# Column sums of exp(phi) by VectorE in place of a block of ones, with a list of side units for each period

## The chip, the cores and the metric

The kernel runs on one core of one Trainium2 chip. The metric is the device time of one execution in microseconds, the median of several runs. Before the change it is 239.88 us (three runs, 239.66 to 240.74).

The core has a matrix engine (TensorE, PE in the profile; its weight loads are PEld), a vector engine (VectorE, DVE), a scalar engine (ScalarE, ACT), GpSimd (POOL) and DMA queues. Matmul results go to PSUM, which this kernel manages as eight banks.

## What is computed

Attention with 32 memory slots for each of 8 batches and 8 heads, and then a bilinear feed-forward layer over all 4608 tokens:

```python
def _attn_ref(q, k, v, phi):                     # q, k, v: (8, 8, 576, 64); phi: (8, 8, 576, 32)
    a = phi - np.max(phi, axis=2, keepdims=True)
    a = np.exp(a)
    a = a / (np.sum(a, axis=2, keepdims=True) + 1e-09)
    k_m = np.einsum('bhsm,bhsd->bhmd', a, k)
    v_m = np.einsum('bhsm,bhsd->bhmd', a, v)
    scores = scale * np.matmul(q, k_m.transpose(0, 1, 3, 2))
    ...                                          # softmax over the 32 slots
    return np.matmul(attn, v_m)

def _moe_ref(x, w_a, w_b, w_out):                # 4608 x 512, d_ff = 1536
    return (x @ w_a) * (x @ w_b) @ w_out
```

The softmax over the sequence (axis 2) divides by the column sums of exp(phi). These are the sums that the change computes in another way.

## The kernel before

The 576 tokens of a batch are laid out as 64 partitions times NI = 9 blocks, with two heads one above the other on the 128 partitions, so NHP = 4 head pairs. `exp_phi` (L194, two halves z) makes exp(phi) in float16. `kv_sums` (L205 to L219) multiplies it with k, v and a third block, which was filled once with 1/16 (`kv_sb`, 2 buffers by batch parity, third index 0 k, 1 v, 2 ones). Each of its 72 matmuls uses a 64x32 tile of the array and 192 columns: 64 for k, 64 for v, and 64 equal ones for the column sums; eight tiles work side by side. `take_kv` (L228, L233) takes the reciprocal of one of these columns and scales k_m and v_m into `rep`. A DMA transpose (`kv_turn`) or TensorE (`kv_transpose`) makes `kvT`. From it `scores` (L297, 32x32 tiles) and `fold` (L368, 64x32 tiles) work: fold multiplies v_m into the two first weight matrices, a third of the 1536 columns at a time (v0, v1, v2), and `take_fold` (L381) copies the results to `vab`, by ScalarE and VectorE. Batches 0 and 1 use a separate path (`sums`, L260), which the change leaves alone.

The long loop is `ups`: for each batch, in two halves of tokens, 12 blocks of d_ff. `up_half` (L633) makes pa and pb (two matmuls of 288 columns each); ScalarE copies pa to `a_sb` (L641), VectorE multiplies it with pb into `ht` (L644). So a batch has 24 slots, a "period". After each slot come two things: `work.advance()`, which pulls some matmuls of the down projection (py, pv, px, L505; written as seven products for two token blocks, on sums `h_sums` that GpSimd makes, L487), at a rate planned for each half, and one entry of a list of side units. These are written out by hand as strings: units joined by + run in one slot, - is an empty slot, a prime means the next batch and _ the one before. The names: exp0/exp1 exp_phi; qt0 to qt3 transposes of q on VectorE (L203); kv and km0/km1 `kv_sums` and `take_kv`; kvt, kvd the transposes; sc, e0, e1 scores and their exponentials; ed, sm0, sm1, tn0, tn1, ad the normalisation by tokens (from batch 4); den, nr the other normalisation; v0, x0a, x0b `fold` and `take_fold` of the first third; L a load of inputs two batches ahead of the one named in the list; d3 means that three more matmuls of the down projection are pulled here.

In period b the unprimed units belong to batch b + 1 and the primed ones to batch b + 2. Before, period 2 has its own list, periods 3 to 5 share one (`every`), period 6 has `last`, and period 7 none.

PSUM banks are handed out in the order in which they were freed; scores, fold and kv_sums hold theirs (4, 4 and 2) until they have been read. Before sc and v0, `settle` pulls down-projection matmuls until one of their banks is free. Each engine executes its own instructions in order, and the loads are issued from GpSimd's queue.

Of the kernel before, what the change touches and what calls it, by code (L numbers as in the profile page):

```python
# [8 lines left out]
F32 = mybir.dt.float32  # L9
F16 = mybir.dt.float16  # L10
AF = mybir.ActivationFunctionType
ALU = mybir.AluOpType

P = 128
CS = 16.0
# [3 lines left out]
def kernel(  # L19
# [11 lines left out]
    nc = tc.nc  # L31

    B, H, S, D = q.shape
    M = phi.shape[3]
    d_model, d_ff = moe_w_a.shape
    NHP = H // 2
# [6 lines left out]
    consts = ctx.enter_context(tc.tile_pool(name="consts", bufs=1))  # L43
# [29 lines left out]
    phis, qs, kvs = {}, {}, {}  # L73
    kv_sbs = [consts.tile([P, 3, NHP, NI * D], F16, name=f"kv_sb{t}") for t in range(2)]

    def load_phi(b):
        phis[b] = inp.tile([P, NHP, NI * M], F32, name="phi_sb")
        nc.gpsimd.dma_start(out=phis[b], in_=rows(phi, b))

    def load_k(b, hps=slice(0, NHP)):  # L80
        kvs[b] = kv_sbs[b % 2]
        nc.gpsimd.dma_start(out=kvs[b][:, 0, hps], in_=rows(k, b)[:, hps])

    def load_v(b, hps=slice(0, NHP)):
        nc.gpsimd.dma_start(out=kvs[b][:, 1, hps], in_=rows(v, b)[:, hps])

    def load_q(b, hps=slice(0, NHP)):
        if b not in qs:
            qs[b] = inp.tile([P, NHP, NI * D], F16, name="q_sb")
        nc.gpsimd.dma_start(out=qs[b][:, hps], in_=rows(q, b)[:, hps])  # L90

    def load(b):
        load_phi(b)
        load_k(b)
        load_v(b)
        load_q(b)
# [48 lines left out]
    banks = Banks()  # L145
# [29 lines left out]
    for x in "o0 o1 p k q0 o2 o3 q1 v0 v1 o4 o5".split():  # L175
        loads[x]()

    attn = {}
    vabs = {}

    def head(g, j):

        jj = j ^ g
        return jj % 2, 2 * g + jj // 2

    def units(b):

        u = {}
        t = {}
# [10 lines left out]
        def q_transpose(hp):  # L200
            if hp == 0:
                t["qT"] = mid.tile([P, NHP, NI * D], F16, name="qT")
            nc.vector.transpose(out=t["qT"][:, hp, :].bitcast(F32), in_=qs[b][:, hp, :].bitcast(F32))  # L203

        def kv_sums():  # L205

            t["pkv"] = [banks.take([P, 3, D], F32, "pkv", hold=True) for _ in range(2)]
            for i in range(NI):
                for g in range(2):
                    for j in range(4):  # L210
                        r, hp = head(g, j)
                        nc.tensor.matmul(  # L212
                            t["pkv"][g][0][32 * j:32 * j + 32],
                            t["exp"][64 * r:64 * r + 64, hp, i, :],
                            kvs[b][64 * r:64 * r + 64, :, hp, D * i:D * (i + 1)],
                            start=(i == 0),
                            stop=(i == NI - 1),
                            tile_position=(64 * r, 32 * j),
                        )  # L219

        def take_kv(gs=range(2)):

            if gs[0] == 0:
                t["rep"] = mid.tile([P, 6, P], F16, name="rep")
                t["rphi"] = small.tile([P, 2], F32, name="rphi")
            for g in gs:
                pkv, bank = t["pkv"][g]
                nc.vector.reciprocal(out=t["rphi"][:, g:g + 1], in_=pkv[:, 2, 0:1])  # L228
                km = pkv[:, 0].rearrange("p (d e) -> p e d", e=2).unsqueeze(2).to_broadcast([P, 2, 4, 32])
                vm = pkv[:, 1].unsqueeze(1).to_broadcast([P, 2, D])  # L230
                for out, x in ((t["rep"][:, 2 * g:2 * g + 2].rearrange("p e (z d) -> p e z d", z=4), km),
                               (t["rep"][:, 4 + g].rearrange("p (z d) -> p z d", z=2), vm)):
                    nc.vector.tensor_scalar(out=out, in0=x, scalar1=t["rphi"][:, g:g + 1], scalar2=None, op0=ALU.mult)  # L233
                banks.free(bank)
# [149 lines left out]
        def one(f, *a):  # L384
            return lambda: f(*a)

        for z in range(2):
            u[f"exp{z}"] = one(exp_phi, z)
            u[f"ks{z}"] = one(sums, z, 0)
            u[f"kt{z}"] = one(transpose, z, 0)  # L390
            u[f"vs{z}"] = one(sums, z, 1)
            u[f"vt{z}"] = one(transpose, z, 1)
            u[f"s{z}"] = one(scores, (z,))
            u[f"e{z}"] = one(exp_scores, z)
            u[f"km{z}"] = one(take_kv, (z,))
            u[f"den{z}"] = one(denominators, z)
            u[f"nr{z}"] = one(normalise, z)
            for hf in range(2):
                u[f"den{z}{hf}"] = one(denominators, z, (hf,))
                u[f"nr{z}{hf}"] = one(normalise, z, slice(hf, hf + 1))  # L400
            for n in range(NCH):
                u[f"v{n}{'ab'[z]}"] = one(fold, 512 * n, 512 * (n + 1), (z,))
                u[f"x{n}{'ab'[z]}"] = one(take_fold, 512 * n, 512 * (n + 1), z)
            for n in range(2):
                u[f"hv{n}{'ab'[z]}"] = one(fold, 256 * n, 256 * (n + 1), (z,))
                u[f"hx{n}{'ab'[z]}"] = one(take_fold, 256 * n, 256 * (n + 1), z)
        for n in range(NCH):
            u[f"v{n}"] = one(fold, 512 * n, 512 * (n + 1), (0, 1))
        for x in range(4):
            u[f"qt{x}"] = one(q_transpose, x)  # L410
        u["sc"] = one(scores, (0, 1))
        u["kv"] = one(kv_sums)
        u["km"] = one(take_kv)
        u["kvt"] = one(kv_transpose)
        u["kvd"] = one(kv_turn)
# [230 lines left out]
    def up(b, i, hfs):  # L646
        for hf in hfs:
            up_half(b, i, hf, 0)
        if len(hfs) > 1:
            yield  # L650
        for hf in hfs:
            up_half(b, i, hf, 1)
        yield

    def ups(steps, side=()):

        side = iter(side)
        for step in steps:
            for _ in up(*step):
                work.advance()  # L660
                next(side, us[step[0]]["-"])()
        for f in side:
            work.advance()
            f()
# [5 lines left out]
    def half_steps(b, hf, lo=0):  # L670

        return [(b, i, (hf,)) for i in range(lo, NFF)]

    us = {b: units(b) for b in range(B)}

    def named(b, names):
# [6 lines left out]
    def slots(b, names):  # L683

        def both(fs):
            return lambda: [f() for f in fs]
        def unit(n):
            if n == "fin":
                return lambda: work.pull(-work.done % NFF)
            if n == "L":  # L690
                return lambda: load(b + 2) if b + 2 < B else None
            if n[0] == "y":
                return lambda: some(int(n[1:]))
            if n[0] == "d" and n[1:].isdigit():
                return lambda: work.pull(int(n[1:]))
            return us[b + n.endswith("'") - n.endswith("_")][n.rstrip("'_")]

        return [both([unit(n) for n in x.split("+")]) for x in names.split()]
# [3 lines left out]
    def some(n):  # L702
        for _ in range(n):
            next(early, None)
# [23 lines left out]
    ups(steps(1, 0, 4), slots(1, "- y1+hv1a+hx1a hv1b+hx1b - y3+v1a+x1a y3+v1b+x1b - -"))  # L728
    ups(half_steps(1, 0, 4), slots(1, "- v2a+x2a+v2b+x2b+qt0' - - qt1'+exp0' exp1'+qt2' - kv'+km'+y9"))
    work.plan(S + HALF, 10)  # L730
    ups(half_steps(1, 1, 4), slots(2, "qt3 kvt - sc+e0+e1 - den0+den1+nr0 - v0+nr1+x0a x0b - v1+x1b x1a"))
    second = "v2_+d2+x2a_+x2b_+exp0 - exp1 - kv+km+d2 qt0 d4+qt1+kvt qt2 L+d1+qt3+sc+e0 - d2+v0+e1+x0a+x0b - den0+exp0'+d2 v1+nr0+x1a x1b+d10+exp1' - qt0' v2+x2a+x2b+kv' - den1+km0' km1'+kvd' nr1+qt1' qt2' qt3' - d6"
    every = "exp0' sc+exp1'+e0+d3+e1+v0+x0a+x0b+ed - kv'+km0' km1' - d4+sm0 sm1+tn0+kvd' - tn1+d2 d3 v1+qt0'+x1a+ad d3+L+x1b qt1' - qt2' - v2+x2a+x2b - qt3' - - - - -"
    last = "sc e0+e1+ed - v0+x0b - - sm0 x0a+sm1+tn0 d2+v1+d3+x1b+tn1 - ad+d6 x1a - - - - v2+x2a - - - - - x2b"
    for b in range(2, B):
        if b == 2:
            load(4)
        names = second if b == 2 else every if b + 2 < B else last
        side = slots(b + 1, names) if b + 1 < B else []
        for hf in range(2):  # L740
            work.plan(S * b + HALF * hf, NFF)
            ups(half_steps(b, hf), side[NFF * hf:NFF * (hf + 1)] if hf == 0 else side[NFF:])
# [30 lines left out]
```

The softmax here doesn't subtract the row's maximum and nothing guards it: scores larger than these inputs give would overflow.

## Time and profile before

| | before |
|---|---|
| device time, median of 3 | 239.88 us (239.66 to 240.74) |
| span of the profiled execution | 237.7 us |
| granted TensorE clock | 1.0 |
| pkv matmuls (kv_sums), 432 | 5.9 us as a group, first at 60.3 us, last at 158.3 us |
| pa and pb matmuls, 768 | 75.8 and 74.9 us |
| VectorE ht multiplies, 168 | 72.0 us, 446 ns each |
| VectorE qT transposes, 32 | 14.6 us, 464 ns each |
| VectorE take_kv: rep and rphi | 8.9 us and 1.9 us |
| GpSimd h_sums, 70 | 46.2, 23.0 and 23.0 us |

The profile is one execution. Matmul durations in it are modelled and overlap, so the time that a group of matmuls really occupies is read from its start to the start of the next group. The kv_sums of batches 2 to 7 start at 60.3, 77.2, 93.1, 104.4, 130.0 and 157.6 us, so periods 2 to 5 begin near 70, 100, 126 and 154 us. Idle time of an engine other than TensorE matters only where TensorE waits for it.

### The profile page before, as it was taken

The numbers are of one execution on the slowest core, as the hardware profiler recorded it, in microseconds if no ns is written. First come the engines' busy times: TensorE is split into PE (matmuls) and PEld (weight loads), VectorE is DVE, ScalarE is ACT, GpSimd is POOL, SyncE is SP. The second block draws the span as 40 slices with busy tenths as digits, with TensorE's granted clock in tenths as the row PEclk, the third lists the DMA queues.
The fourth block names the chain that finished last, engine by engine and source line by source line (L and its number), as shares of the span: only waits on it lengthen the run. The fifth ranks groups of instructions, "written<-read, shape, count | busy, mean of one in ns | idle before, by whom it ended". The sixth has DMA issues, their size and how long they took to land.

```text
span 237.7 us, 7733 instructions
## 1 busy us (share of the span) xinstructions
PE 228.5 (96%) x3070; PEld 168.0 (71%) x3070; DVE 169.1 (71%) x414; ACT 153.1 (64%) x394; POOL 154.9 (65%) x132
## 2 busy tenths in 40 slices
PE   7968999999999999999999999999999999999993
PEld 7734664456756867867787877867787778888882
DVE  4635784469949968989766888689767776756642
ACT  2266671669699488786878458766876777465330
POOL 7953244599979949592979599682919265946001
PEclk9999999999999999999999999999999999999999
DMA  6999999999975999743799548997333342032145
GB/s 233 238 197 206 206 258 207 248 216 276 227 172 143 202 285 224 163 97 77 173 224 211 109 104 191 213 171 125 57 87 66 75 89 52 17 76 65 39 110 143
DMA packets 38437, 37.27 MB, mean 157 GB/s; under 512 B 14689, under 2 KB 32481, under 8 KB 38401
## 3 DMA queue, kind: packets, MB, share of 16 engines
q0 software_dynamic: 19264, 23.14, 52.5%
q1 hardware_dynamic: 18624, 12.85, 23.8%
q10 hardware_dynamic: 512, 0.79, 0.9%
q8 instruction: 24, 0.39, 0.6%
q14 instruction: 13, 0.10, 0.1%
HBM read 42.47 MB, written 9.44 MB: 218 GB/s over the span
## 4 chain that ended last, share of the span: by engine, by line
PE 90%; DMA 3%; ACT 2%; DVE 2%; issue 2%; DVEq 0%; POOLq 0%
PE pa L633 21%; PE pb L633 20%; PE py L505 18%; PE pv L505 9%; PE pva L368 6%; PE po L429 5%; PE px L505 4%; DMA phi_sb<-in_phi_dram 3%; PE pkv L212 2%; PE pscore L297 2%; PE pk L260 1%; PE pw L151 1%; DVE ht L644 1%; PE pD L320 1%; ACT L L321 1%
## 5 line engine op out<-in xcount | busy, mean ns | idle before, releaser
L644 DVE TENSOR_TENSOR ht<-a_sb,pb 128x288 f16<-128x288 f16 x168 | 72.0, 446 | 33.2 <-ACT a_sb L641 24.6
L633 PEld LDWEIGHTS <-vab 128*128 128x128 f16 x768 | 72.2, 98 | 25.9 <-issue 7.8
L641 ACT CAST a_sb<-pa 128x288 f16<-128x288 f32 x168 | 65.7, 410 | 31.3 <-PE pa L633 28.1
L633 PE MATMUL pb<-A,vab 128*128 128x288 f16 x384 | 74.9, 286 | 1.0 <-ACT vab L381 0.5
L633 PE MATMUL pa<-A,vab 128*128 128x288 f16 x384 | 75.8, 287 | 0.1
L487 POOL TENSOR_TENSOR h_sums<-ht 128x768 f16<-128x768 f16 x28 | 46.2, 1654 | 26.3 <-DVE ht L644 26.3
L505 PEld LDWEIGHTS <-h_sums 128*128 128x128 f16 x384 | 37.1, 98 | 7.6 <-issue 1.3
L381 ACT CAST vab<-pva 128x512 f16<-128x512 f32 (+1 forms) x60 | 31.9, 579 | 7.3 <-PE pva L368 7.0
L505 PEld LDWEIGHTS <-ht 128*128 128x128 f16 x288 | 27.9, 98 | 5.9 <-issue 0.9
L381 DVE CAST vab<-pva 128x512 f16<-128x512 f32 (+1 forms) x44 | 26.9, 637 | 5.7 <-PE pva L368 5.7
L505 PE MATMUL py<-w_sums,h_sums 128*128 128x256 f16 x192 | 30.5, 273 | 0.0
L487 POOL TENSOR_TENSOR h_sums<-h_sums,ht 128x768 f16<-128x768 f16 x14 | 23.0, 1645 | 1.0
L487 POOL TENSOR_TENSOR h_sums<-ht,h_sums 128x768 f16<-128x768 f16 x14 | 23.0, 1640 | 0.9
L310 ACT ACTIVATE E<-pscore 128x288 f16<-128x288 f32 x32 | 10.9, 417 | 9.0 <-PE pscore L297 8.8
L505 PE MATMUL py<-w_sums,ht 128*128 128x256 f16 x96 | 16.2, 273 | 0.1
L512 ACT ACTIVATE u<-py 128x256 f32<-128x256 f32 x32 | 12.4, 387 | 5.3 <-PE py L505 4.9
L505 PE MATMUL pv<-w_sums,h_sums 128*128 128x256 f16 x96 | 15.7, 273 | 0.0
L505 PE MATMUL py<-wo_sb,ht 128*128 128x256 f16 x96 | 15.7, 273 | 0.0
L505 PE MATMUL px<-wo_sb,ht 128*128 128x256 f16 x96 | 15.2, 273 | 0.0
L203 DVE STREAM_TRANSPOSE qT<-q_sb 128x288 f32<-128x288 f32 x32 | 14.6, 464 | 0.2 <-DMA q_sb<-in_q_dram 0.2
L505 PE MATMUL pv<-wo_sb,h_sums 128*128 128x256 f16 x96 | 14.4, 273 | 0.0
L194 ACT ACTIVATE exp_sb<-phi_sb 128x576 f16<-128x576 f32 x16 | 10.8, 689 | 5.4 <-DMA phi_sb<-in_phi_dram 5.4
(70 smaller groups left out, 265.1 us busy)
## 6 DMA issues: line engine op xcount, KB each, us to landing
out_dram<-o_sb SPq DMA_DIRECT2D x68, 128.0 KB, 2.4
phi_sb<-in_phi_dram POOLq DMA_DIRECT2D x8, 576.0 KB, 7.0
kv_sb<-in_v_dram POOLq DMA_DIRECT2D x7, 576.0 KB, 11.8
kv_sb<-in_k_dram POOLq DMA_DIRECT2D x7, 576.0 KB, 9.7
q_sb<-in_q_dram POOLq DMA_DIRECT2D x6, 576.0 KB, 14.5
wo_sb<-in_moe_w_out_dram POOLq DMA_DIRECT2D x6, 256.0 KB, 13.7
q_sb<-in_q_dram POOLq DMA_DIRECT2D x4, 288.0 KB, 9.6
wa_sb<-in_moe_w_a_dram POOLq DMA_DIRECT2D x2, 512.0 KB, 13.8
```

What stands on the lines that cost most here:

```text
L194: nc.scalar.activation(out=t["exp"][:, 2 * z:2 * z + 2, :, :], in_=phis[b][:, 2 * z:2 * z + 2, :].rearrange("p c (i m) -> p c i m", m=M), ...
L203: nc.vector.transpose(out=t["qT"][:, hp, :].bitcast(F32), in_=qs[b][:, hp, :].bitcast(F32))
L310: nc.scalar.activation(out=Ev[:, g, :, z, :], in_=pss, func=AF.Exp, scale=1.0 / (8.0 * CS))
L368: nc.tensor.matmul(t["pva", lo, z][g][0][32 * j:32 * j + 32, 0:hi - lo], t["kvT"][64 * r:64 * r + 64, 4 + g, M * j:M * j + M], w_sbs[z][64 ...
L381: engine_copy(out=vabs[b][z][:, g, lo:hi], in_=pva[:, 0:hi - lo])
L429: nc.tensor.matmul(po, ht[:, i, P * c:P * (c + 1)], wo_sb[:, i, :], start=(i == 0), stop=(i == NFF - 1))
L487: engine.tensor_tensor(out=out, in0=in0, in1=in1, op=op)
L505: nc.tensor.matmul(po, lhs[:, i], rhs[:, i], start=first and i == 0, stop=i == KH - 1, skip_group_check=not first)
L512: nc.scalar.mul(out=x, in_=po, mul=scale)
L633: nc.tensor.matmul(ps, vabs[b][x][:, g, P * i:P * (i + 1)], attn[b][:, g, HALF * hf:HALF * (hf + 1)], start=(g == 0), stop=(g == 1))
L641: nc.scalar.copy(out=a_sbs[b, i, hf], in_=ps)
L644: nc.vector.tensor_tensor(out=ht[:, i, t0:t0 + HALF], in0=a_sbs.pop((b, i, hf)), in1=ps, op=ALU.mult)
```

## The change

For batches 4 to 7, `slot_sums` lets VectorE add up exp(phi) over the nine blocks, for two head pairs at a time (ps0, ps1), in float32. The result `es` lies in the first part of the third block of `kv_sb`, whose ones are no longer needed. `kv_sums` then streams only k and v (128 columns in place of 192) and ends with eight float32 matmuls of one column that add `es` over the 64 partitions with the scale 1/16 (`one_cs`). `take_kv` reads the sum from column 128. The purpose is to take work off TensorE that VectorE can do.

Second, each period gets a list of its own: ps units are added, many units move by some slots, v0 and kv' come together in periods 4 and 5, v0 is split in period 3, pulls of the down projection are spread anew, and loads are named by batch (L4 to L7).

```diff
+    one_cs = consts.tile([P, 1], F32, name="one_cs")
+    nc.vector.memset(one_cs, 1.0 / CS)
...
+        def slot_sums(z):
+            if z == 0:
+                t["es"] = kvs[b][:, 2, 0, 0:2 * NHP * M].bitcast(F32).rearrange("p (c m) -> p c m", m=M)
+            nc.vector.tensor_reduce(out=t["es"][:, 2 * z:2 * z + 2], in_=t["exp"][:, 2 * z:2 * z + 2].rearrange("p c i m -> p c m i"),
+                                    axis=mybir.AxisListType.X, op=ALU.add)
+
         def kv_sums():
-            t["pkv"] = [banks.take([P, 3, D], F32, "pkv", hold=True) for _ in range(2)]
+            given = "es" in t
+            n = (3 - given) * D
+            t["pkv"] = [banks.take([P, 2 * D + (1 if given else D)], F32, "pkv", hold=True) for _ in range(2)]
...
-                            t["pkv"][g][0][32 * j:32 * j + 32],
+                            t["pkv"][g][0][32 * j:32 * j + 32, 0:n],
                             t["exp"][64 * r:64 * r + 64, hp, i, :],
-                            kvs[b][64 * r:64 * r + 64, :, hp, D * i:D * (i + 1)],
+                            kvs[b][64 * r:64 * r + 64, 0:3 - given, hp, D * i:D * (i + 1)],
...
+            for g in range(2 * given):
+                for j in range(4):
+                    r, hp = head(g, j)
+                    nc.tensor.matmul(
+                        t["pkv"][g][0][32 * j:32 * j + 32, 2 * D:2 * D + 1],
+                        t["es"][64 * r:64 * r + 64, hp],
+                        one_cs[64 * r:64 * r + 64],
+                        start=True,
+                        stop=True,
+                        tile_position=(64 * r, 32 * j),
+                    )
...
-    ups(half_steps(1, 1, 4), slots(2, "qt3 kvt - sc+e0+e1 - den0+den1+nr0 - v0+nr1+x0a x0b - v1+x1b x1a"))
-    second = "v2_+d2+x2a_+x2b_+exp0 - exp1 - kv+km+d2 qt0 d4+qt1+kvt qt2 L+d1+qt3+sc+e0 - d2+v0+e1+x0a+x0b - den0+exp0'+d2 v1+nr0+x1a x1b+d10+exp1' - qt0' v2+x2a+x2b+kv' - den1+km0' km1'+kvd' nr1+qt1' qt2' qt3' - d6"
-    every = "exp0' sc+exp1'+e0+d3+e1+v0+x0a+x0b+ed - kv'+km0' km1' - d4+sm0 sm1+tn0+kvd' - tn1+d2 d3 v1+qt0'+x1a+ad d3+L+x1b qt1' - qt2' - v2+x2a+x2b - qt3' - - - - -"
-    last = "sc e0+e1+ed - v0+x0b - - sm0 x0a+sm1+tn0 d2+v1+d3+x1b+tn1 - ad+d6 x1a - - - - v2+x2a - - - - - x2b"
+    ups(half_steps(1, 1, 4), slots(2, "qt3 kvt - sc+e0+e1 - den0+den1+nr0 - v0+nr1+x0a x0b - v1+x1a+x1b -"))
+    period = {}
+    period[2] = "d1+exp0+L4+v2_+x2a_+x2b_+qt0 - exp1 - kv+km - qt1+d7+kvt+d1 d7+L5+qt2+qt3+sc+e0 - - d1+v0+e1+x0a+x0b+d2 - exp0'+ps0'+den0+d4 v1+nr0+x1a x1b+d10+exp1'+ps1' - - - v2+kv'+x2b+x2a den1+km0' km1'+kvd'+qt0' - nr1+d4 qt1'+d6+d6+qt2' - d2+qt3'"
+    period[3] = "exp0' sc+exp1'+ps0'+ps1'+e0+e1+d1+ed - v0a+x0a+kv'+km0' - v0b+x0b+km1' L6+d5+sm0+sm1 - - d6+d5+kvd'+tn1 - tn0 qt0' v1+ad+d3+x1a - - - - v2+d2+x1b+x2a+x2b d4 - qt1' d1 - qt2'+qt3'"
+    period[4] = "exp0'+d4 sc+exp1'+ps0'+ps1'+e0+e1+d4+ed - v0+x0a+x0b+kv'+km0' d6+km1' - kvd'+d5+d5+sm0 qt0'+tn0+sm1 - - d3+d2+tn1 ad qt1'+v1a+v1b+x1a+d3 L7 - - - x1b v2a+v2b+x2a+x2b qt2' - d2 - - qt3'"
+    period[5] = "exp0' sc+exp1'+ps0'+ps1'+e0+e1+d3+ed - v0+x0a+x0b+kv'+d2+km0' d7+km1' - d5+d3+sm0+tn0 - sm1 d4+tn1+kvd' d5 - ad+d3+qt0' v1+x1a - - x1b - v2+x2b+qt1' - - x2a+qt2'+qt3' d2 - -"
+    period[6] = "sc e0+e1+ed - v0+x0b - - sm0 x0a+sm1 d2+v1+d7+tn0+x1b+tn1 - d6+x1a ad d3 - - - - v2+x2a - d1+x2b - - -"
+    period[7] = ""
     for b in range(2, B):
...
-        names = second if b == 2 else every if b + 2 < B else last
-        side = slots(b + 1, names) if b + 1 < B else []
+        side = slots(b + 1, period[b])
```

More of the change, by code (lines that the diff above doesn't have):

```diff
@@ L227, in take_kv @@
                 pkv, bank = t["pkv"][g]
-                nc.vector.reciprocal(out=t["rphi"][:, g:g + 1], in_=pkv[:, 2, 0:1])
-                km = pkv[:, 0].rearrange("p (d e) -> p e d", e=2).unsqueeze(2).to_broadcast([P, 2, 4, 32])
-                vm = pkv[:, 1].unsqueeze(1).to_broadcast([P, 2, D])
+                nc.vector.reciprocal(out=t["rphi"][:, g:g + 1], in_=pkv[:, 2 * D:2 * D + 1])
+                km = pkv[:, 0:D].rearrange("p (d e) -> p e d", e=2).unsqueeze(2).to_broadcast([P, 2, 4, 32])
+                vm = pkv[:, D:2 * D].unsqueeze(1).to_broadcast([P, 2, D])
                 for out, x in ((t["rep"][:, 2 * g:2 * g + 2].rearrange("p e (z d) -> p e z d", z=4), km),
@@ L388, in units @@
             u[f"exp{z}"] = one(exp_phi, z)
+            u[f"ps{z}"] = one(slot_sums, z)
             u[f"ks{z}"] = one(sums, z, 0)
@@ L689, in unit @@
                 return lambda: work.pull(-work.done % NFF)
-            if n == "L":
-                return lambda: load(b + 2) if b + 2 < B else None
+            if n[0] == "L":
+                return lambda: load(int(n[1:]))
             if n[0] == "y":
@@ L730 @@
     work.plan(S + HALF, 10)
-    ups(half_steps(1, 1, 4), slots(2, "qt3 kvt - sc+e0+e1 - den0+den1+nr0 - v0+nr1+x0a x0b - v1+x1b x1a"))
-    second = "v2_+d2+x2a_+x2b_+exp0 - exp1 - kv+km+d2 qt0 d4+qt1+kvt qt2 L+d1+qt3+sc+e0 - d2+v0+e1+x0a+x0b - den0+exp0'+d2 v1+nr0+x1a x1b+d10+exp1' - qt0' v2+x2a+x2b+kv' - den1+km0' km1'+kvd' nr1+qt1' qt2' qt3' - d6"
-    every = "exp0' sc+exp1'+e0+d3+e1+v0+x0a+x0b+ed - kv'+km0' km1' - d4+sm0 sm1+tn0+kvd' - tn1+d2 d3 v1+qt0'+x1a+ad d3+L+x1b qt1' - qt2' - v2+x2a+x2b - qt3' - - - - -"
-    last = "sc e0+e1+ed - v0+x0b - - sm0 x0a+sm1+tn0 d2+v1+d3+x1b+tn1 - ad+d6 x1a - - - - v2+x2a - - - - - x2b"
+    ups(half_steps(1, 1, 4), slots(2, "qt3 kvt - sc+e0+e1 - den0+den1+nr0 - v0+nr1+x0a x0b - v1+x1a+x1b -"))
[6 more added lines that the diff above has]
+    period[7] = ""
     for b in range(2, B):
-        if b == 2:
-            load(4)
-        names = second if b == 2 else every if b + 2 < B else last
-        side = slots(b + 1, names) if b + 1 < B else []
+        side = slots(b + 1, period[b])
         for hf in range(2):
```

## The prediction

> **What bounds the kernel now.** I read the page from the top: the busy row, the 40 slices, then the chain of work that ended last.
>
> ```profile
> PE 228.5 (96%) x3070; PEld 168.0 (71%) x3070; DVE 169.1 (71%) x414; ACT 153.1 (64%) x394; POOL 154.9 (65%) x132
> ...
> PE   7968999999999999999999999999999999999993
> ...
> PE 90%; DMA 3%; ACT 2%; DVE 2%; issue 2%; DVEq 0%; POOLq 0%
> ```
>
> TensorE is busy in every slice from the fifth to the last but one and makes up 90% of the chain. The DMA, ScalarE and VectorE shares lie mostly before 60 us, which the change does not touch. So a microsecond on another engine is worth nothing unless it makes TensorE wait, and a microsecond of TensorE's own work is worth one. A busy TensorE need not be a streaming one, so I went on to its timeline, here at the head of the period that works on batch 4 (columns: start, us, engine, line, ...):
>
> ```profile
> 126.90 0.50 PE L505 MATMUL py<-w_sums,ht 128*128 128x256 f16 x3
> 127.33 0.41 PE L368 MATMUL pva<-wa_sb,kvT 64*32 64x512 f16 x8
> 127.56 0.40 PE L368 MATMUL pva<-wb_sb,kvT 64*32 64x512 f16 x8
> 127.89 0.42 PE L633 MATMUL pa<-A,vab 128*128 128x288 f16 x2
> ...
> 129.20 0.82 PE L505 MATMUL py<-wo_sb,ht 128*128 128x256 f16 x6
> 129.95 0.94 PE L212 MATMUL pkv<-kv_sb,exp_sb 64*32 64x192 f16 x72
> 130.82 0.42 PE L633 MATMUL pa<-A,vab 128*128 128x288 f16 x2
> ```
>
> A run of six py of 256 columns goes from 137.70 to 138.36, 0.110 us each, so close to 2.4 columns per ns with a few ns between (two pa and pb of 288 stand 0.25 us apart, the same). Eight 512-column matmuls on eight tiles stream in parallel and are then due 0.213 us, and start 0.23 apart. Three py should take 0.32 us, but the first pva starts 0.43 after them; the second pva group takes 0.33 instead of 0.213. So **one excursion from 128x128 tiles to small tiles and back costs 0.11 + 0.12 = 0.23 us** beyond its columns. The 72 pkv matmuls are 9 rounds of 192 columns on eight tiles, 0.72 us, and occupy 0.87, the remainder being this cost.
>
> Stalls: from 69 us on, the gaps between groups of matmuls beyond columns and tile changes are few, of about 0.2 us each (pa at 103.66 to pb at 104.10, pa at 156.39 to pb at 156.83, and some four like them), and part may be matmul records missing from the trace. I put the true sum at 0.5 to 1.5 us. That is all a better order can recover.
>
> Last, VectorE in the stretches where the new work goes (us and instructions for PE, PEld, DVE, ACT, POOL):
>
> ```profile
> 100.00:113.00 13.00, 12.97 (x223) 9.29 (x222) 11.39 (x31) 9.44 (x25) 7.90 (x6) 1.00 0.41 86
> 126.00:140.00 14.00, 14.00 (x227) 11.10 (x225) 11.28 (x28) 8.24 (x23) 11.21 (x8) 1.00 0.66 122
> 154.00:166.00 12.00, 11.97 (x206) 8.90 (x205) 10.73 (x28) 8.49 (x23) 6.81 (x5) 1.00 0.96 158
> ```
>
> VectorE has only 1.6, 2.7 and 1.3 us free in the first half of periods 3, 4 and 5.
>
> **What the Trainium skill says.** "TensorEngine Tiling (Array Packing)", Key Properties: changing the tiling mode drains TensorE. The trace agrees, at the 0.23 us above. "FP8 and Floating Point Precision", TensorE Precision Notes: a true FP32 matmul makes four passes. No FP32 matmul is in this trace. "TensorE: Matmul & The Clock Gate", the section on 56 against 53.3 ns: a warm matmul takes its columns over 2.4 GHz plus 2.5 ns, 109.2 ns for 256 (agreed, 110 measured), and starts never come closer than about 25 ns however few the columns. Here 36 matmuls of 64 columns (batch 1's value sums) took 0.38 us with their tile change, so about 7 ns each over four tiles, which is some 27 ns on one tile. "VectorE: DVE Perf Modes", the tier table: tensor_reduce runs only at 1x. Agreed: sum<-E took 812 ns for 640 elements and 674 ns for 512, so 1.08 ns an element.
>
> **The change, part by part.**
>
> 1. Columns of kv_sums, batches 4 to 7: 192 become 128. Nine rounds of 64 columns at 2.4 per ns are 0.24 us each. The first head pairs of batch 1 show it: 36 pk matmuls of 128 columns stand 0.61 us in the chain, 36 of 64 columns 0.38, a difference of 0.23. On TensorE's path: **-0.96 us** for four batches.
>
> 2. Eight one-column FP32 matmuls per batch, on the same tiles, so with no tile change of their own. Not in the trace. Lower end: eight starts at 7 ns, 0.05 us. Upper end: four passes of eight matmuls with nothing overlapped at the skill's 25 ns, 0.8 us. Four passes with the tiles overlapped at 7 ns would be 0.22. I take 0.13, between the two overlapped values, since eight tiles take them in parallel: **+0.5 us** for four batches (0.2 to 3.2).
>
> 3. Eight reductions over 576 elements on VectorE: 674 + 64 x 1.08 = 743 ns each, 5.9 us in all. It is off TensorE's path if VectorE catches up. Behind them queue ht multiplies, which free the pb banks, and the casts of vab. In period 4 the two fit in the idle of VectorE before its vab casts (0.81 us at 127.84) and ht (0.48 at 129.61), which is nearly the 1.49 us wanted; and the new list starts v0 two slots after the scores, so the casts come later. The second reduction waits for exp1', which ran on ScalarE in 101.53 to 102.2 in period 3, while kv' came at 104.4; the sums are ready before the last eight matmuls ask. I cost it at 0 and keep 0 to 2 us for PSUM banks that come late.
>
> 4. Reciprocal and scaling in take_kv keep their shapes and are read from another column: 0. The memset of one column takes under 0.2 us on VectorE before 56 us, at a time when TensorE's work is other: 0.
>
> 5. Small-tile excursions. Before, each of periods 3 to 5 has five: sc, v0, kv', v1, v2. In the new lists for 4 and 5, v0 and kv' stand in one slot with no 128x128 matmul between, so four each. In period 3, v0a shares kv' but v0b is alone: five again. Periods 2 (six) and 6 (four) keep their number. Two fewer at 0.23: **-0.46 us**.
>
> 6. Loads. Batch 6 is issued at slot 6, not 12. Its buffers are free by then (batch 4's sums and transposes are done in period 2). The four issues take 3.05 us of GpSimd's queue, which idled 3.07 us before 109.66 there; h_sums queues behind. Batch 4's load goes a few operations later, and its phi is first used half a period later. All 0.
>
> 7. Slots and pulls of down products move; their number stays. Normalising batch 3's second half (nr1) is one slot later, 1.1 us, with 18 products explicitly pulled from nr1 to the period's end instead of 6, so twelve more, 1.28 us of TensorE work that covers the delay. I credit the new order with half of the recoverable stalls: **-0.5 us** (-1 to +1).
>
> Sum: -0.96 + 0.5 - 0.46 - 0.5 = -1.4 us. 239.88 - 1.4 = **238.5 us**.
>
> **The rivals.**
>
> - *Near nothing, 239.6.* The FP32 matmuls cost 0.22 each batch (+0.88), eating the columns' saving, and no stall is recovered: -0.96 + 0.88 - 0.46 = -0.5, less 0.2 for one late reduction. For it: nothing in the trace measures them. Against: the excursions are counted from the lists.
> - *VectorE becomes the bound, 242.0.* Free time of 1.6 and 1.3 us in periods 3 and 5 barely holds 1.49; sm0, sm1 and tn1 stand in the same half. If half of each pair of reductions reaches TensorE through late banks (0.75 us, three periods, 2.2) and the FP32 matmuls take 0.4 a batch (+1.6) the sum is -0.96 + 1.6 - 0.46 + 2.2 = +2.4; some recovered later, 242.0. Against: VectorE has over 3 us free in the second halves, and TensorE carries products that need no bank from it.
> - *More, 236.9.* FP32 near its lower end (+0.2), all 1.5 us of stalls recovered and the wait around 65 to 70 us, where the last slots of period 1 change, shortened by 0.3: -0.96 + 0.2 - 0.46 - 1.5 - 0.3 = -3.0.
>
> **How the numbers follow.** Forecast 0.46, near nothing 0.27, VectorE bound 0.14, more 0.13. The line of 0.5% is 1.2 us, at 238.68 and 241.08. The forecast lies just under it, so about two thirds of its chance (0.32) falls in faster; more adds 0.13, and near nothing a little (0.03): faster 0.48. VectorE bound gives slower 0.13. The other 0.39 is within. The range goes from 236.8, at the case of more, to 240.8, which takes the upper half of the FP32 cost without its extreme and leaves out most of the VectorE case.
>
> **What the profile after would show.** pkv as 64x128 and a new FP32 group of one column, with the time from the first pkv to the next pa at about 0.74 us in place of 0.87 (0.63 if step 2 is at its lower end, over 0.9 if the near-nothing rival's price is too low). Eight reductions of about 0.74 us. VectorE near 175 us busy, TensorE still the chain's 90%. In periods 4 and 5, pva and pkv back to back with no 0.23 us between. New waits of pa or pb on ht, or of the FP32 matmuls on the reductions, would show the VectorE rival. The forecast is wrong if the FP32 group takes over 0.4 us, if ht falls behind a_sb by more than a slot in periods 3 and 5, or if the waits before 69 us move by more than half a microsecond.

## The result and the profile after

The change makes the kernel slower: 242.64 us (median of 6, 242.55 to 244.51) against 240.02 us for the kernel before, run beside it (median of 6). The ratio is **1.0126, 95% interval 1.0091 to 1.0161**, about 3 us. In the experiments below, the kernel before gave 239.54 to 239.69 us as its median; each is given as a ratio to the runs of before beside it.

The page after, busy row, TensorE by slices, and chain:

```profile
PE 229.4 (95%) x3134; PEld 168.4 (70%) x3134; DVE 176.6 (73%) x423; ACT 153.8 (64%) x394; POOL 154.9 (64%) x132
...
PE   7768999999999999999999999999999999999993
...
PE 85%; DVE 4%; ACT 4%; issue 3%; DMA 3%; DVEq 0%; POOLq 0%
```

TensorE is still busy in every slice from the fifth to the last but one, and the slices alone show almost no change. The chain does: TensorE's share falls from 90% to 85% while those of VectorE, ScalarE and "issue" (time with no wait that the profile shows) each rise. VectorE is busy for 7.5 us more, not the 5.9 forecast. The windows at the head of periods 3 to 5:

```profile
100.00:113.00 13.00, 12.40 (x220) 9.19 (x218) 11.85 (x29) 8.46 (x23) 10.83 (x10) 1.00 0.67 133
126.00:140.00 14.00, 14.00 (x242) 11.38 (x240) 12.58 (x30) 8.88 (x24) 9.97 (x7) 1.00 0.41 91
154.00:166.00 12.00, 11.53 (x216) 8.82 (x214) 10.86 (x24) 8.11 (x21) 6.79 (x5) 1.00 1.05 203
```

TensorE (the second number) now loses 0.6 and 0.5 us in the first and third. I then took the start of every matmul from the two traces, subtracted its columns at 2.4 per ns, and added up what is left from the first pa of batch 2 to the last matmul. That stretch is 161.5 us before and 164.5 after, although the columns fell by the 0.96 us forecast, so what is left beyond the columns grew by about 4 us.

Two tile views of the change show its new work (count; min/median/max duration in ns; first and last start):

```profile
L233 PE MATMUL pkv<-one_cs,kv_sb x64: 160/176/188, 95.6 to 161.8; 64*32 64x1 f32 x64
```

```profile
L210 DVE TENSOR_REDUCE kv_sb<-exp_sb x8: 1122/1142/1157, 88.7 to 158.4; 128x64 f32<-128x576 f16 x8
```

Each of the eight float32 matmuls of a batch appears as two records, so 64 for four batches. A reduction takes 1142 ns, not 743.

The timeline of TensorE around two kv' groups of the change, batch 4 and batch 7 (a note in brackets is idle time and what ended it):

```profile
94.25 0.41 PE L389 MATMUL pva<-wa_sb,kvT 64*32 64x512 f16 x8 [0.19 <-DVE ht L666]
94.61 0.41 PE L389 MATMUL pva<-wb_sb,kvT 64*32 64x512 f16 x8
94.97 0.80 PE L222 MATMUL pkv<-kv_sb,exp_sb 64*32 64x128 f16 x72
95.55 0.33 PE L233 MATMUL pkv<-one_cs,kv_sb 64*32 64x1 f32 x16
95.82 0.42 PE L655 MATMUL pa<-A,vab 128*128 128x288 f16 x2
...
159.66 0.38 PE L389 MATMUL pva<-wb_sb,kvT 64*32 64x512 f16 x1
160.29 0.41 PE L389 MATMUL pva<-wb_sb,kvT 64*32 64x512 f16 x7 [0.26 <-DVE ht L666]
160.41 1.05 PE L222 MATMUL pkv<-kv_sb,exp_sb 64*32 64x128 f16 x72
161.25 0.22 PE L233 MATMUL pkv<-one_cs,kv_sb 64*32 64x1 f32 x2
161.69 0.27 PE L233 MATMUL pkv<-one_cs,kv_sb 64*32 64x1 f32 x14 [0.22 <-issue]
161.88 0.39 PE L527 MATMUL py<-w_sums,ht 128*128 128x256 f16 x2
```

Three things are in these lines. The group of batch 4 has nothing in its way and takes 94.97 to 95.82, **0.85 us, against 0.87 to 0.88 for an undisturbed group of 192 columns before**: the exchange saves TensorE almost nothing even when all goes well. Second, pva waits for ht, VectorE's multiply, which reads pb and so frees a PSUM bank. Third, the float32 group of batch 7 stops for 0.38 us after two matmuls with no engine to wait for.

From the first pkv to the next other matmul, in batches 4, 5, 6 and 7, in us:

| kernel | 4 | 5 | 6 | 7 | sum |
|---|---|---|---|---|---|
| before | 0.88 | 1.01 | 0.87 | 0.88 | 3.64 |
| after | 0.85 | 1.29 | 1.13 | 1.47 | 4.74 |

**Theories.** A: the new sums cost the time, by VectorE's reductions (banks come late) and by the float32 group. B, the rival: the new lists cost it. C, beside A: TensorE's supply of instructions. The page shows an instruction queue of 24 packets:

```profile
q8 instruction: 24, 0.39, 0.7%
```

0.39 MB over 24 is 16 KB each. TensorE has 6155 instructions in the trace before, so some 256 to a packet. The Trainium skill, "Runtime: NRT & Kernel Launch", Instruction fetch mechanics, says that engines refill their instructions in 16 KiB blocks of 256, mostly hidden. The packet size here agrees; whether the refill is hidden is what theory C doubts. Counting TensorE's instructions from 0 at the start of the trace, the unexplained stalls of the change end at numbers 2497 (83.8 us, 0.4 us long), 3009 (100.7 us, 0.6) and 4801 (161.7 us, 0.4): 512 and 1792 apart, both multiples of 256, and each 2.3 to 2.4 us after a packet of that queue began. All three numbers are 449 + 256 k, with k = 8, 10 and 17. The stall at 3009 lies in the middle of a plain pair of pb:

```profile
99.99 0.29 PE L655 MATMUL pb<-A,vab 128*128 128x288 f16 x1
100.73 0.30 PE L655 MATMUL pb<-A,vab 128*128 128x288 f16 x1 [0.45 <-issue]
```

### The profile page after: what moved, and what is told of

The parts are those of the page before. It is cut to its first block, busy times and chain, and to the rows that moved or that the text cites. A ratio compares the mean times of both kernels' runs of the same rounds, so it can differ in the third digit from the quotient of the medians.

```text
span 241.0 us, 7870 instructions
## 1 busy us (share of the span) xinstructions
PE 229.4 (95%) x3134; PEld 168.4 (70%) x3134; DVE 176.6 (73%) x423; ACT 153.8 (64%) x394; POOL 154.9 (64%) x132
## 4 chain that ended last, share of the span: by engine, by line
PE 85%; DVE 4%; ACT 4%; issue 3%; DMA 3%; DVEq 0%; POOLq 0%
PE pa L655 19%; PE pb L655 19%; PE py L527 17%; PE pv L527 8%; PE pva L389 5%; PE po L451 5%; PE px L527 3%; DMA phi_sb<-in_phi_dram 3%; PE pscore L318 2%; PE pkv L222 2%; DVE ht L666 1%; PE pk L281 1%; ACT E L331 1%; PE pw L151 1%; DVE o_sb L538 1%
## 5 line engine op out<-in xcount | busy, mean ns | idle before, releaser
L663 ACT CAST a_sb<-pa 128x288 f16<-128x288 f32 x168 | 66.6, 411 | 34.1 <-PE pa L655 30.8
L527 PE MATMUL py<-wo_sb,ht 128*128 128x256 f16 x96 | 16.2, 273 | 0.0
L527 PE MATMUL pv<-w_sums,h_sums 128*128 128x256 f16 x96 | 16.2, 273 | 0.0
L527 PE MATMUL pv<-wo_sb,h_sums 128*128 128x256 f16 x96 | 14.9, 273 | 0.0
```

The costliest lines, as they stand in the source:

```text
L527: nc.tensor.matmul(po, lhs[:, i], rhs[:, i], start=first and i == 0, stop=i == KH - 1, skip_group_check=not first)
L663: nc.scalar.copy(out=a_sbs[b, i, hf], in_=ps)
```

## The experiments

**1. New lists alone.** Edit: the ps units do nothing, so `kv_sums` streams the ones again.

```diff
         def slot_sums(z):
-            if z == 0:
-                t["es"] = ...
-            nc.vector.tensor_reduce(out=t["es"][:, 2 * z:2 * z + 2], ...)
+            pass
```

> The new lists with the old block of ones for all batches (the ps units do nothing, kv_sums streams 192 columns, no float32 matmuls). Theory A, the new sums cost the time (float32 matmuls on TensorE, 1.14 us reductions on VectorE that let banks come late): the new lists alone are no slower than the kernel before, about 239.5 us, since they have two small-tile excursions fewer. Theory B, the lists cost it (order of the units, v0 next to kv'): about 242 us, as with the whole change. Theory C, stalls in TensorE's supply of instructions at every 256th instruction, set off by bursts of small matmuls: between, 240 to 241.5, with a stall of 0.3 us or more that has no wait on an engine.

Measured: 239.46 us, ratio 1.0007 (0.9987 to 1.0027). Theory B falls. The lists do have 46 tile changes from batch 2 on where before has 50, the two excursions fewer that were counted, and yet give no measurable gain. In this trace a stall of 0.46 us at instruction 1985 (449 + 6 x 256) and a wait of the scores for `kvT` of 0.3 us at 102 us can account for what the two excursions should have gained.

**2. New sums in the old lists.** ps0', ps1' put right after exp0', exp1' in the lists of before, the rest as changed.

> The new sums (reductions, 128 columns, float32 matmuls) in the lists of before, with ps0, ps1 put right after exp0, exp1. Theory A: slower than before by 1 us or more, 241 us or more: the matmul group of each batch is no shorter than before (0.85 against 0.87 us undisturbed) and VectorE's 9.2 us of reductions delay ht. Theory B: about 240 us, no difference. Theory C: anything from 240 to 241.5, since bursts stay apart by 128x128 matmuls and stalls fall elsewhere.

Measured: 244.62 us, ratio 1.0205 (1.0190 to 1.0219), about 5 us slower, which is on theory A's side (1 us or more) and far outside those of B and C. Three of its waits on TensorE:

```profile
90.93 0.40 PE L655 MATMUL pb<-A,vab 128*128 128x288 f16 x2 [0.86 <-DVE ht L666]
94.58 0.41 PE L389 MATMUL pva<-wb_sb,kvT 64*32 64x512 f16 x8 [0.34 <-DVE ht L666]
104.61 0.48 PE L318 MATMUL pscore<-qT,kvT 32*32 32x288 f16 x32 [0.99 <-DMA kvT<-rep]
```

The new lists are what makes the new sums bearable: without them the same sums cost 2% and not 1.3%. The third line is a wait that before did not have, the scores of batch 4 for the transposed `kvT`. The transpose is issued 1.8 us later than before (99.9 against 98.1 us), behind VectorE's `rep`, and takes 4.7 us from issue to landing in place of 2.9; why it lands more slowly is open.

**3. One pass and not two.** Sums and constant in float16.

```diff
-    one_cs = consts.tile([P, 1], F32, name="one_cs")
+    one_cs = consts.tile([P, 1], F16, name="one_cs")
...
-                t["es"] = kvs[b][:, 2, 0, 0:2 * NHP * M].bitcast(F32)...
+                t["es"] = kvs[b][:, 2, 0, 0:NHP * M]...
```

> The change with the sums and the constant in float16, so each small matmul is one pass and not two. If the float32 passes cost their visible 0.17 us a batch, of which half would go, and 32 fewer pairs of instructions shorten the burst: 0.3 to 0.5 us faster than the change, about 242.2 us, by theory A; by theory C the stalls at the instruction blocks also move, and up to 1.2 us go or come.

Measured: 241.19 us, ratio 1.0070 (1.0053 to 1.0087), about 1.4 us better than the change and so more than the passes. Undisturbed, the group of batch 4 now takes 0.74 us (0.85 with float32), 0.11 us a batch, 0.4 us in all:

```profile
94.56 0.80 PE L223 MATMUL pkv<-kv_sb,exp_sb 64*32 64x128 f16 x72
95.15 0.23 PE L234 MATMUL pkv<-one_cs,kv_sb 64*32 64x1 f16 x8
95.31 0.42 PE L656 MATMUL pa<-A,vab 128*128 128x288 f16 x2
```

The other 1 us fits theory C: with 16 entries of TensorE fewer in each of the four batches, its trace has no stall at 3009 or 4801. The reductions stay at 1140 ns.

**4. Short reductions.** The sum over one block of nine (the column sums are those of one block).

```diff
-            ... in_=t["exp"][:, 2 * z:2 * z + 2].rearrange("p c i m -> p c m i"),
+            ... in_=t["exp"][:, 2 * z:2 * z + 2, 0:1].rearrange("p c i m -> p c m i"),
```

> The change with the reduction taken over one block of nine only (64 elements in place of 576 in each instruction; the column sums are those of one block). VectorE is relieved of about 8 x 1.0 us, TensorE's work is the same. Theory A with VectorE as the cause: 1.0 to 1.6 us faster than the change, about 241.3 us, without the waits of pb, pva and pa on ht at 90 to 94, 107 and 160 us. If VectorE hardly matters: within 0.4 us of the change, 242.4 us.

Measured: 241.43 us, ratio 1.0074 (1.0055 to 1.0092), 1.2 us better than the change, as theory A had it. The waits on ht at 90 to 94, 107 and 160 us are gone. Two stalls at instruction blocks stay, at 3009 (0.6 us) and 4801 (0.8), and a new wait appears that the change had hidden. From its list of waits (engine, tile and line, what it waited for, us in total, times, longest):

```profile
PE pa L655 <- DMA A<-E: 0.7, 1, 0.7
```

**5. The step of the reduction.** Nine neighbouring elements in place of nine 64 bytes apart.

```diff
-  t["exp"][:, 2 * z:2 * z + 2].rearrange("p c i m -> p c m i")
+  t["exp"][:, 2 * z:2 * z + 2].rearrange("p c i m -> p c (i m)").rearrange("p c (m i) -> p c m i", i=NI)
```

> The change with each reduction taken over nine neighbouring elements in place of nine 64 bytes apart (same number of elements and outputs; the sums are of the wrong elements). If the step of 64 bytes is what makes a reduction take 1.14 us, it falls to about 0.74 us (sum<-E's 1.08 ns an element) and the time falls by a third to a half of what the tiny reduction gained (1.2 us): about 242.1 us. If the length is set by the 64 outputs or the float32 result, it stays 1.14 us and the time that of the change, 242.6.

The reductions now take what the prediction had priced:

```profile
L210 DVE TENSOR_REDUCE kv_sb<-exp_sb x8: 743/746/753, 88.8 to 157.5; 128x64 f32<-128x576 f16 x8
```

So the step of 64 bytes costs 1142 - 746 = 396 ns an instruction. The Trainium skill has a reason on "SBUF — State Buffer", Door 1: SBUF has lines of 16 bytes, and each access that crosses to a new one pays. That this is the cause was not tried beyond the two steps. Measured: 241.59 us, ratio 1.0086 (1.0064 to 1.0107), better than the change by about 0.4%, though the intervals overlap.

**6. The place of the instruction blocks.** 32 warm-up matmuls fewer at the start, in the change and, as a control, in the kernel before.

```diff
-    fill(64, P)
-    chain(0, "exp0 exp1 f18 ks0 ...
+    fill(48, P)
+    chain(0, "exp0 exp1 f2 ks0 ...
```

> The change with 32 warm-up matmuls fewer at the start, where TensorE waits for phi anyway (64 instructions fewer ahead of everything). Theory C: the stalls without an engine to wait for (0.4 us at 83.4, 0.6 at 100.0, 0.4 at 161.3 in the change) do not stay at their matmuls: the ones that remain lie again at instructions 449 + 256 k, now 64 instructions later in the program, and as the kv' groups no longer end there, up to 1.2 us go, 241.4 us. Without theory C: the stalls stay at the same matmuls and the time is that of the change, 242.6.

> Control: the kernel before with the same 32 warm-up matmuls fewer. The kernel before shows one such stall of 0.2 us in its later part, so theory C expects a change of at most 0.4 us either way, 239.4 to 240.2; a gain of 1 us here as well would say that the warm-up itself and not the place of the instruction blocks is what moved the other kernel.

Measured: the change so shifted 241.35 us, ratio 1.0071 (1.0057 to 1.0084), 1.3 us better; before so shifted 240.56 us, 1.0037 (1.0024 to 1.0051), 0.9 us worse, where at most 0.4 was expected. In the shifted change all three stalls are gone and no other one of 0.3 us lies at a block from batch 2 on; the very float32 group that stopped now runs through, while the wait on VectorE just before it stays:

```profile
159.37 0.41 PE L389 MATMUL pva<-wb_sb,kvT 64*32 64x512 f16 x7 [0.24 <-DVE ht L666]
159.49 1.00 PE L222 MATMUL pkv<-kv_sb,exp_sb 64*32 64x128 f16 x72
160.28 0.33 PE L233 MATMUL pkv<-one_cs,kv_sb 64*32 64x1 f32 x16
160.55 0.39 PE L527 MATMUL py<-w_sums,ht 128*128 128x256 f16 x2
```

Matching every matmul of the change with the same one of the shifted change shows where the time went. At 45 us the two traces are level within 0.2 us. Of the 1.45 us that the shifted one then gains, 1.3 fall at three places: 83.8 us (0.2), 100.7 us (0.6) and 161.7 us (0.5), the three stalls.

The 14 traces of this case say more. With packets and block ends both counted from 0, instruction 449 + 256 k never starts sooner than 2.19 us after packet k began, in 322 crossings. From 60 us on, 15 gaps of 0.3 us or more lie just before such an instruction and are not ordinary changes of tile; all of them end 2.2 to 2.5 us after their packet began. So TensorE stops where it reaches such a number before that time is up. What makes a packet begin late was not tried.

Theory C holds for the change. The control missed its forecast: it excludes that fewer warm-ups are a gain by themselves, but its own loss comes from elsewhere. Its granted clock was half for 3.4 us at the start, but by 36.7 us its trace is level with that of before. Then VectorE waited 1.05 us for the transposed E before the token sums at 109.8 us, and pb then 0.38 us for ht; 0.8 us are lost there. That transpose was issued 1.1 us later than before and took 4.9 us to land in place of 3.2, and why stays open.

**7. The sums by pairs.** Four float16 additions in place of each reduction, float16 small matmuls.

```diff
+            for out, in0, in1 in ((h[:, c], x[:, c, 0:4], x[:, c, 4:8]), (h[:, c, 0:2], h[:, c, 0:2], h[:, c, 2:4]),
+                                  (h[:, c, 0], h[:, c, 0], h[:, c, 1]), (t["es"][:, c], h[:, c, 0], x[:, c, 8])):
+                nc.vector.tensor_tensor(out=out, in0=in0, in1=in1, op=ALU.add)
```

> The change with the nine blocks added pairwise in float16 by four tensor_tensor (256, 128, 64 and 64 outputs) for each reduction, and float16 small matmuls. From h_sums on VectorE (550 ns for 768 elements, two an ns or so) and its fixed part I expect 0.27, 0.2, 0.17, 0.17 us, 0.8 us in place of 1.14 for each z. If VectorE's time is what costs, this is 0.3 to 0.6 us faster than the float16 variant of 241.2, about 240.7 us; if the number of VectorE instructions costs, no faster than 241.2.

Measured: 262.95 us, ratio 1.0979 (1.0956 to 1.1001), over 20 us slower where a gain was forecast. The timeline of VectorE and GpSimd:

```profile
88.54 1.45 DVE L215 TENSOR_TENSOR kv_sb<-exp_sb 128x256 f16<-128x256 f16 x1
89.91 1.63 POOL L513 TENSOR_TENSOR h_sums<-h_sums,ht 128x768 f16<-128x768 f16 x1
90.02 2.81 DVE L215 TENSOR_TENSOR kv_sb<-kv_sb 128x128 f16<-128x128 f16 x2
91.51 1.27 POOL L356 TENSOR_TENSOR A<-E,R 128x576 f16<-128x576 f16 x1
...
98.11 0.29 DVE L215 TENSOR_TENSOR kv_sb<-exp_sb 128x256 f16<-128x256 f16 x1 [1.10 <-ACT exp_sb L196]
98.43 0.45 DVE L215 TENSOR_TENSOR kv_sb<-kv_sb 128x128 f16<-128x128 f16 x2
```

With GpSimd idle, the four additions take 0.29, 0.23, 0.19 and 0.19 us, 0.9 in all and close to the forecast; beside GpSimd's additions, each lasts until a GpSimd instruction ends, up to 1.6 us. The Trainium skill states it on the same page, "SBUF — State Buffer", in "SBUF: two separate sides": a VectorE instruction with two SBUF inputs and a GpSimd one that reads SBUF share a pair of ports, and one blocks the other for its whole length. The reductions, with one input, kept their 1.14 us beside GpSimd.

**8. Reductions that nobody reads.** Experiment 1 with the eight reductions made into a float16 scratch.

> The new lists with the block of ones (239.5 us by itself), and the eight reductions made as well, into a float16 scratch that nothing reads. It costs VectorE's 9.2 us alone. If those reach TensorE through late PSUM banks as the tiny reduction said (it gained 1.2 us), 240.3 to 241.0 us, with waits of pb and pva on ht near 90, 93 and 159 us. If they only cost where the sums are waited for, 239.5 us.

Measured: 241.50 us, ratio 1.0088 (1.0064 to 1.0112), somewhat above the range. From 1.0007 to 1.0088 is **1.9 us for VectorE's work alone**, with TensorE's program as it was. Matched matmul by matmul with the trace of the new lists alone, the delay comes in steps: at pb, pva and pkv from 90.7 to 95.1 us (1.0 us), at pa and pva from 107.0 to 108.8 us (0.6), at pkv at 131.9 us (0.2) and at pva at 159.8 us (0.6). Each step stands behind the reductions of one batch. The group of batch 5 takes 1.31 us here, as in the change (1.29), without any float32 matmul and without a wait for the sums: pa after it waits for ht. The wait of pva at the head of period 5 is there again, with nothing of the sums in it:

```profile
159.75 0.41 PE L389 MATMUL pva<-wb_sb,kvT 64*32 64x512 f16 x7 [0.24 <-DVE ht L666]
```

**9. Both costs off, and a load.** Float16 sums over one block only (the column sums are those of one block); and the same with batch 6's load moved.

```diff
-    period[3] = "... L6+d5+sm0+sm1 ... v1+ad+d3+x1a - - - - v2+d2 ..."
+    period[3] = "... d5+sm0+sm1 ... v1+ad+d3+x1a L6 - - - v2+d2 ..."
```

> The change with float16 sums and with the reduction over one block of nine only (the column sums are those of one block): what is left is the saving of the columns and the new lists. If VectorE's reductions (1.2 us) and the float32 passes with their stalls (1.4 us) add up, 242.6 - 2.6 = 240.0 us or less; columns by themselves save 0.13 us a batch against the new lists alone (239.5), so 239.0 us if nothing else waits. If the wait for the transposed A at the end of period 3 (0.7 to 0.9 us in the variants with short reductions) shows, 239.9 us.

> The same, and the load of batch 6 moved from slot 6 to slot 14 of period 3, behind the transpose that makes A. In the kernel before, A landed 3.2 us after its issue, in the change and its variants 10.3 to 11.4 us, with the load in flight. Theory: the landing falls back to about 3 us, the wait of pa for A disappears, and the time is 0.5 to 0.9 us below f16_tiny, 239.0 us. If the load has nothing to do with it, the two are equal.

Measured: 239.80 us, 1.0009 (0.9991 to 1.0027), and 240.88 us, 1.0043 (1.0027 to 1.0058). The first closes the account: with short reductions and float16 sums, the change is back at the time of before. Its trace has no stall at a block end from 60 us on either, so all three costs are off. In the execution that was traced, more than the narrower groups save is spent on one wait, of the scores for `kvT`, 1.3 us:

```profile
PE pscore L319 <- DMA kvT<-rep: 1.3, 1, 1.3
```

The transpose took 2.9 us to land in the kernel before and 5.2 here; why is open.

The second missed. A did land sooner, from issue to landing 4.8 us in place of 10.2 (3.2 in the kernel before), so the load was in its way. But the time rose by about 0.8 us (0.34%) where a gain was forecast. The traced execution is the slowest of its 18 (243.02 us, mean granted clock 0.975), so its waits are not a measure of the median. In it the load's four issues hold GpSimd's queue from 119.74 to 122.78, with h_sums behind it, and pv stood still for 1.4 us at 133.5 to 135.0. The profile puts that to h_sums. It also ends at instruction 4033, 449 + 14 x 256, 2.45 us after packet 14 began. The weight load that waits for h_sums had already run at 133.47:

```profile
133.47 0.10 PEld L528 LDWEIGHTS <-h_sums 128*128 128x128 f16 x1
135.00 0.81 PE L528 MATMUL pv<-w_sums,h_sums 128*128 128x256 f16 x6 [1.25 <-POOL h_sums L510]
```

And in the trace of the first variant the same pv starts while the h_sums addition named here is still running (131.85 to 133.49 us there):

```profile
132.09 0.82 PE L528 MATMUL pv<-w_sums,h_sums 128*128 128x256 f16 x6
```

So this stall belongs to the block end, and the name in brackets is only the semaphore that came last. What cost the other executions their 0.8 us is not known.

**10. One piece taken from the change.** The kernel before, with v0 beside kv' in periods 3 to 5.

```diff
-    every = "exp0' sc+exp1'+e0+d3+e1+v0+x0a+x0b+ed - kv'+km0' km1' - ...
+    every = "exp0' sc+exp1'+e0+d3+e1+ed - v0+x0a+x0b+kv'+km0' km1' - ...
```

> The kernel before, with one thing taken from the change: in periods 3 to 5, v0 and its copies move from slot 1 to slot 3, next to kv'. Each of the three periods has one excursion to small tiles fewer, 0.23 to 0.25 us: 0.7 us faster, 238.9 us, if nothing else waits; 239.6 or more if the later copies of v0 meet take_kv on VectorE and hold banks.

Measured: 239.19 us, ratio **0.9981 (0.9970 to 0.9992)**, about 0.45 us faster than before (0.2 to 0.7) and so faster than both kernels. The forecast of 0.7 lies at the end of that interval. Something of it is lost in period 3, where kv' starts late:

```profile
103.89 0.51 PE L368 MATMUL pva<-wb_sb,kvT 64*32 64x512 f16 x8
104.48 0.94 PE L212 MATMUL pkv<-kv_sb,exp_sb 64*32 64x192 f16 x72
```

The second pva group should last 0.23 us, and pkv starts 0.59 after it. Banks still held would explain that, which was not tried.

## Why the prediction was wrong

The forecast was 1.4 us faster and the result is 3.0 us slower, a difference of 4.4 us. The ratios lay the 1.26% out in a row: new lists 0.07, with reductions 0.88 (plus 0.81, 1.9 us), with 128 columns and float16 matmuls 0.70 (minus 0.18, 0.4 us, within the noise of the two ratios), with float32 1.26 (plus 0.56, 1.3 us). Of the last step, the shifted change gives back 0.55 with its float32 matmuls still there (1.0071), so nearly all of it is the place of the block ends and little is float32 itself. Set beside the prediction's terms:

| | forecast, us | measured, us |
|---|---|---|
| new lists (steps 5 and 7) | -0.96 | +0.2 |
| reductions (step 3) | 0 | +1.9 |
| narrower groups and small matmuls (steps 1 and 2) | -0.46 | -0.4 with float16 |
| stalls at block ends, with what float32 adds | no term | +1.3 |

The third line agrees only because the saving and the cost were both priced too high, so it is luck. Point by point:

- **What bounds the kernel**: right. Every loss is time in which TensorE waits.
- **Step 1, columns, -0.96 us**: right in columns, mis-sized in time. 72 pkv matmuls of 128 columns take 0.57 to 0.63 us from first to last start, not the 0.48 of nine rounds. In batch 4 of the change the first three rounds of eight take 55 ns each (53 by columns). From the 34th on they start one by one, 8 or 9 ns apart, so some 66 ns for eight. The pk groups that gave the price had only 36 matmuls. The trace of before had the longer case: the 72 pk matmuls of 64 columns at 14.79 us take 0.58 us, as long as 72 of 128 columns here, and the second 36 of them also start 8 or 9 ns apart. Why the starts thin out after some 35 matmuls is open. With the float16 matmuls the saving is 0.13 us a batch, with float32 0.02.
- **Step 2, float32 matmuls, 0.13 us a batch**: mis-sized. Undisturbed, first to last start is 0.17 us, 0.27 with the change of tiles; the trace shows two records for each matmul, where the page cited by the prediction says four passes. Disturbed, it is up to 0.65, beyond the 0.4 us that the prediction named as a sign of being wrong. The disturbance was not in the sum at all: 0.2 us for the second reduction in batch 5, and the instruction block in batch 7.
- **Step 3, reductions at 0**: this is the step that failed. The length was taken from sum<-E, which reads neighbouring elements: 743 against 1142 ns. And the idle time of VectorE that was to take them was counted per window, while pb, pva and pa want their banks within a microsecond or two: 1.9 us reached TensorE, in the places listed under experiment 8. The range kept for it, 0 to 2, did hold it; the overall range, whose upper end left out most of the VectorE case, did not.
- **Step 4**: nothing seen against it.
- **Step 5, two excursions fewer**: right as a count (50 to 46 tile changes with the lists alone), and experiment 10 shows that such a move can pay; in the new lists other waits cancelled it. One reading behind the price was loose: the 0.15 us that a pkv group occupies beyond its columns is only the way back, since the way in lies before its first start.
- **Step 6, loads at 0**: wrong. The earlier load of batch 6 made A land 10.3 us after its issue in place of 3.2. In the change this was still hidden; where the other waits were taken away it showed, 0.7 us.
- **Step 7, stalls recovered, -0.5 us**: wrong, the lists alone gain nothing and the change adds stalls.
- **The rivals**: the VectorE case, 242.0 us at a chance of 0.14, was the right one in mechanism (pb and pva waiting on ht) and nearly in size, the latter in part by luck: its 1.6 us for float32 stand where the stalls took 1.3. What spoke against it, over 3 us free in the second halves, does not help banks wanted in the first. No rival had the instruction blocks, the 1.3 us for which the prediction has no term.

## What to carry to other kernels

Where TensorE is full, work moved off it to an engine that is busy 81 to 89% of the same stretch is not free: price it by how long that engine holds back the PSUM banks in those few microseconds, and take the duration from a row with the same access pattern. Before counting a saving in columns, compare the group's time with its number of matmuls, for a group of many small ones can be bound by starts (here 8 or 9 ns each). And when a change of program length moves the time, count instructions: a stall can belong to a place in the instruction stream and not to the matmul where it shows.

## What was not expected of the hardware

- TensorE stopped for 0.2 to 1.4 us at instructions 449 + 256 k, each time until 2.2 to 2.5 us after the start of a 16 KB instruction packet. 64 instructions fewer at the start removed three such stalls (1.3 us).
- In an unbroken run of 72 matmuls on 64x32 tiles, those after the first 35 or so started one by one, 8 or 9 ns apart, with 64 columns (batch 0) as with 128 (batch 4 of the change).
- A VectorE addition with two SBUF inputs took 0.19 us alone and up to 1.6 us beside GpSimd; a reduction with one input was not touched.
- A step of 64 bytes made a float16 reduction of 576 elements take 1142 ns in place of 746.
